# An RWKV-7 and GELU kernel: channel sums two heads per matmul, and another order of its first tasks

## The chip, the cores and the metric

The kernel runs on one core of a Trainium2 chip. The metric is the device time of one execution in microseconds, taken as the median of several runs. The engines are TensorE (PE, with its weight loads PEld), VectorE (DVE), ScalarE (ACT), GpSimd (POOL) and SyncE (SP), whose queue issues nearly all transfers between main memory and the core.

## The reference

An RWKV-7 recurrence over 768 steps for 4 batches and 8 heads of width 40, then an MLP with a quick GELU over the 3072 tokens (8 heads of 40 make 320 inputs, 2048 hidden):

```python
for t in range(S):
    y[:, :, t] = np.einsum('bhd,bhde->bhe', rt, state)
    Sa = np.einsum('bhde,bhe->bhd', state, at)
    state_decay = state * wt[:, :, None, :] - np.einsum('bhd,bhe->bhde', Sa, bt)
    state = state_decay + np.einsum('bhd,bhe->bhde', vt, kt)
...
x = np.ascontiguousarray(attn_out.transpose(0, 2, 1, 3)).reshape(B * S, H * D)
h = x @ w_in
g = h * (1.0 / (1.0 + np.exp(-1.702 * h)))
return (g @ w_out).astype(np.float32)
```

## The kernel before

The recurrence is worked in 24 units: 12 chunks of 64 steps, each for two pairs of batches (16 heads' worth of work per unit, b a batch of the pair). For each unit the logarithms of the decays w are summed over time, and exponentials of the sums scale a, k, b and r (`decay`, `prep`). Sums by time come from a matmul (`by_time`, tile ps_cum). Sums by channel come for the first four units (`BY_PE = 4`) from matmuls too (`by_channel`, tile ps_cumc), for the others from scans on VectorE over a second copy of w (tile wc). Then come products of the scaled factors (tiles ps_A, ps_N, ps_RV), the inverse of a triangular matrix in five levels (`inverse`: matmuls into ps_level, a copy on ScalarE or VectorE, L794, a transpose on VectorE, L733, and so on; the result is T), the solution and the state (`solve`: ps_B, ps_X, the product M on VectorE, ps_y, then x). x goes to main memory and comes back in another layout (x_dram, xT_all). Every two units give one chunk of the MLP (`mlp`): up-projections into ps_up, GELU on ScalarE, down-projections into ps_down.

The MLP's weights come as eight pieces of 1280 columns in 64-bit form, four transfers each, and are brought to 32 bits in the kernel (`weight`): a pass on ScalarE (L457), three on VectorE (L461, L465, L469), a join on GpSimd (L473). Their raw bytes land in places that other data uses later: extra, w_sb, xT_all.

All this is cut into 2709 tasks, and the string ORDER lists them by hand in one sequence: the number of the task, a letter for its engine (p, a, d, g, s), and for tasks that use PSUM a bank. Each engine takes its tasks in this order. For a transfer (s) the digit is a window: the queue waits until at most so many transfers, among all before, are still under way.

```python
def transfer(t, dst, src, queue=nc.sync):
    begun.append(queue.dma_start(dst, src).ins)
    if t.window and len(begun) > t.window:
        tc.add_manual_dep(begun[-1], begun[-1 - t.window].name, ...)
```

Tiles rotate: two buffers for a with k, b, r with v; three for the log decays (logw) and for wc. A load into a buffer waits for the readers of what was in it.

Of the kernel before, what the change touches and what calls it, by code (L numbers as in the profile page):

```python
# [109 lines left out]
0s 8s 1s4 5s 102a 7s 6s 3a 9s 157a 87p0 88p1 10s 89a1 100p2 90a0 95d 13s4 4a 11s 93d 12s 101d2 98p3 2s 94d 97d 17s 103p1 16s 96d  # L110
142p0 15s 104a1 105d1 141p2 143a0 106d 99d3 107p1 144a2 18s4 148g 132p3 108a1 109d1 155p0 45s4 149d 27s 150g 156d0 158p2 14s4
110p1 159a2 160d2 91s4 130p0 161d 19a 24s4 112d1 162p2 111a1 22d 26s4 25s 163a2 113p1 20d 131a0 152g 164d2 34s4 92a 272s 21d
165p0 114a1 151g 271s 147a 153p2 115d1 273s 166a0 167d0 116p1 23g 28a 154d2 262p0 343s 117d1 263p2 133a3 342s 264a2 118d1 168p3
36s 31d 33s 119p1 276g 169a3 170d3 35s 120d1 42s 122a1 171p2 277d 278g 121a 43s 124d1 123a1 126p3 173d2 125a1 127d3 285a 29d
128p1 172a2 44s4 286p3 30d 54s4 37a 174p2 129d1 32g 51s4 288d3 134p1 178a2 146s4 175d2 145s 265a0 135d1 176a 187p0 289d 136p1
275s4 179a2 266g 61s 38d 138d1 188a0 341s 139s 287a3 181p0 39d 185p3 40d 137a1 177a2 290p1 313d 180a2 182a0 53s4 280g 279g 274s
186a3 183p2 292d1 281p0 291a1 333p3 41g 184d2 332p1 282d0 189p2 334a3 60s4 345s 314p0 190d2 316a0 346d 355a 191p3 347d 315d0
193d3 356p2 344s2 62s 140s 194s 195s4 192d3 293p0 335a1 358d2 46a 283p3 359d 317p1 294a0 295d0 349g 318a1 284d3 360p0 269a 348d
350g 296p1 336d 361a0 362d0 319p3 383d 357a2 297a1 298d1 384p0 321p2 49d 320a3 299p1 385a0 47d 322a2 63s4 363p3 300a1 301d1
323d2 386a0 302p1 364a3 365d3 353p0 351p2 306a1 48d 267s3 207p3 52s3 307a1 305d1 208p3 50g 268s3 64a 303d1 209p3 352d2 210p3  # L120
211p3 354d0 308a1 196p2 304a 212p3 65d 197p2 213p3 72s3 214p3 70s3 270d 55a 309p1 337s3 198p2 69s4 366p0 310a1 66d 199p2 367a0
200p2 58d 468p1 201p2 368d0 469a 473s 202p2 476s 203p2 67d 387p0 477s 470a1 490d 204p2 68g 480s 339a 205p2 369p1 388d0 206a2
215p3 371d1 218p0 219p0 56d 472s4 216p3 483g 71s4 220p0 217a3 471d 81s4 221p0 482d 79s 311p2 222p0 370a1 223p0 224p0 312d2 225p0
340d 372p3 229p1 478s4 376a3 230p1 57d 378a3 324p2 560s4 377a3 59g 226p0 78s4 375a3 325d2 231p1 73a 232p1 227p0 373d3 326p2 374d
228a0 389p3 484g 479s3 327d2 338s4 240p0 529d 390a3 481g 328d2 379p3 233p1 380a3 329d 234p1 391p2 485g 241p0 556s4 392d2 80s4
242p0 393d2 74d 486p3 235p1 487d3 530p2 236p1 75d 531a2 381p3 237p1 532a2 330s4 382d3 238p1 76d 491p2 394p3 494a2 493d2 77g
239a1 243p0 395d3 82a 488p1 557s3 396p3 489d1 474a 558s4 83d 331s 251p1 492d2 495d 252p1 84d 85d 253p1 398d3 86g 559s4 548p2
244p0 703s 397d3 549a 570d 553s 245p0 496d 550a2 552s 399d 497a 254p1 551g 554a 498p3 564d 400s 568p2 565g 499a3 246p0 569d2
500d3 563g 247p0 562d 694p2 561g 255p1 248a0 401s2 249d0 475d 256p1 250s 533p3 257p1 534a3 555d 695a 571p0 535p3 573d0 258p1
574a0 698s4 501d 696a2 609d 502g 536a3 537p2 572d0 259a1 576d 566p3 538a2 702s 402p0 575g 567d3 577a 403p0 404p0 539d2 785s3  # L130
700a 405p0 706s 708d 406p0 578p3 407p0 580d3 408p0 260d1 610p2 409p0 581d 709g 410p0 611d2 411p0 612d2 503p1 707d 582g 412a0
424p2 425p2 504d1 704s2 426p2 505d1 427p2 697d 428p2 579d3 613p1 701d 429p2 614a1 583p0 430p2 584a0 506d 431p2 585d0 432p2 507a
782s2 586d 433p2 587d 446p3 434a2 508p1 588p0 509a1 447p3 590d0 589a0 510d1 261s2 413p2 511d 699s 414p2 591d 512a 783s 415p2
592g 416p2 513p0 417p2 514a0 515d0 593p1 516d 418p2 594a1 595d1 419p2 596d 420p2 517a 597d 421p2 422p2 518p0 423a2 435p1 519d0
436p1 521d0 520g 437p1 522d0 438p1 523d0 439p1 440p1 524d0 525p2 716p0 526a2 441p1 717d0 927s 442p1 718d0 527p2 443p1 719d0
444p1 528d2 598p0 721d 445a1 540p2 720d 722g 601d0 603a0 617p1 602d0 541d2 448p3 618a1 604d0 542p2 619d1 599d0 600d 615p1 705s
544d2 449p3 616a1 781s 710d 545g 711d 605p0 723p1 606a0 450p3 607p0 451p3 546s 608d0 930s 452p3 725d1 724d1 620p0 726d 543d2
727a 773p1 453p3 621d0 778s 774a 547s 754d 728p2 622p0 454d3 455d3 729d2 456s 457p3 775a1 776g 730d2 784s 786g 779a 777s 624d0
458p3 623d0 625g 731d 793p1 833d 732a 459p3 733p2 789g 460p3 626s 734a2 794d1 735d2 714p0 790g 736d 461p3 780d 737g 1009s 918p1
755p2 923s 462p3 715d0 756a2 627s 757a2 788d 463p3 738p0 787d 464p3 739a0 740d0 919a 795p2 465d3 758p0 1006s 466d3 798a2 921d  # L140
650p3 467s 759d0 920a1 651p3 924a 928s 796d2 712p1 797d2 652p3 922s 800d 799g 653p3 932d 801a 654p3 834p0 655p3 713d1 656p3
657p3 835d0 760p2 836d0 925d 658p3 761a2 659p3 762p1 660a3 741d 628p0 742d 926s 629p0 630p0 763d1 802p2 764d1 631p0 803a2 804d2
632p0 805d 633p0 806a 743p3 634p0 746d3 635p0 747d3 837p1 931g 748d3 636p0 838a1 1007s 749d3 637p0 807p2 744d3 933g 638a0 639p1
808d2 640p1 791p3 745a 809d2 672p0 810d 792d3 811a 750p2 641p1 751a2 812p3 642p1 813a3 814d3 752p2 643p1 753d2 644p1 815d 645p1
816a 765p3 839p2 766d3 646p1 840a2 647p1 817p3 648p1 818a3 819d3 767p2 820d 649a1 821d 673p0 769d2 929s 768d2 770g 822p3 934d
674p0 825a3 826a3 940p1 827a3 675p0 1151s 828a3 935d 943a1 771s 661p2 823d3 662p2 941d1 1154s 824a 663p2 942d1 997p3 945d 944g
664p2 998a 1002s 978d 938p1 946g 665p2 939d1 666p2 772s 667p2 668p2 829p1 669p2 999a3 1000d 1001s 830d1 670p2 1003a 1011d 676p0
671a2 1004d 831p3 841p1 677p0 832d3 1005s 842d1 936p3 843d1 678p0 937d3 844p2 679p0 845d2 947p1 1010g 680d0 846p3 948a1 681d0
1012d 682s 683p2 847d3 1013g 1008s 848d3 1019p0 1014g 949d1 684p2 1022a0 1230s 849d 1233s 979p3 685p2 980a3 950d 850s 1020d0
981a3 951g 1142p1 1021d0 686p2 1024d 1143a 1147s 1023d 1025g 982p3 1057d 687p2 1152s 952p0 851s 983a3 1145g 688p2 1156d 1146s  # L150
953a0 954d0 984p3 1144a1 955d 1148a 689p2 956d 985a3 1149d 986p0 690p2 987a0 1150s 988d0 957p1 691a2 863p3 958a1 692d2 864p3
959d1 865p3 693s 960d 866p3 961d 1026p0 867p3 1027a0 1028d0 868p3 1029d 1155g 869p3 1157d 1030a 1058p2 870p3 871p3 1059a2 872p3
# [97 lines left out]
def rwkv7_gelu_quick(ctx: ExitStack, tc: tile.TileContext, time_d, v_d, w_d, wc_d, ak_d, b_d, rv_d, w_in, w_out, out):  # L250
# [125 lines left out]
    for t in logw_t:  # L376
        nc.gpsimd.memset(t[:, DM:], 0.0)
# [772 lines left out]
```

## Time and profile before

| | us |
|---|---|
| median of 3 runs | 681.54 (681.05 to 681.87) |
| the profiled execution's own time | 679.49 |
| its span | 677.7 |
| TensorE busy | 649.6 (96%) |
| VectorE busy | 449.7 (66%) |
| ScalarE busy | 329.1 (49%) |
| GpSimd busy | 175.7 (26%) |
| mean granted TensorE clock | 0.994 of full |

The span runs from the first to the last instruction; the profiled execution is one run, and the 1.8 us between its time and its span lie around the instructions. Busy time of TensorE holds matmuls at whatever pace they run. Durations in the timelines are those of merged rows, so neighbouring rows of one engine overlap by their pipelining.

### The profile page before, as it was taken

The numbers are of one execution on the slowest core, as the hardware profiler recorded it, in microseconds if no ns is written. First come the engines' busy times: TensorE is split into PE (matmuls) and PEld (weight loads), VectorE is DVE, ScalarE is ACT, GpSimd is POOL, SyncE is SP. The second block draws the span as 40 slices with busy tenths as digits, with TensorE's granted clock in tenths as the row PEclk, the third lists the DMA queues.
The fourth block names the chain that finished last, engine by engine and source line by source line (L and its number), as shares of the span: only waits on it lengthen the run. The fifth ranks groups of instructions, "written<-read, shape, count | busy, mean of one in ns | idle before, by whom it ended". The sixth has DMA issues, their size and how long they took to land.

```text
span 677.7 us, 42447 instructions
## 1 busy us (share of the span) xinstructions
PE 649.6 (96%) x19616; PEld 568.7 (84%) x19616; DVE 449.7 (66%) x916; ACT 329.1 (49%) x681; POOL 175.7 (26%) x201
## 2 busy tenths in 40 slices
PE   5777999999999999999999999999999999999997
PEld 4667787787999997888888899999889798799896
DVE  5777779777867668757776687868656766675001
ACT  3676745634564655654545445455344454263010
POOL 6541443324123123123113211322411421300000
PEclk9979999999999999999999999999999999999999
DMA  6875753415324314432404513513412411200200
GB/s 208 295 255 160 226 172 97 129 42 152 107 64 131 94 58 124 114 107 65 124 14 131 149 35 108 155 33 107 140 38 62 130 53 45 69 15 14 60 13 21
DMA packets 35473, 69.74 MB, mean 103 GB/s; under 512 B 5472, under 2 KB 14816, under 8 KB 35296
## 3 DMA queue, kind: packets, MB, share of 16 engines
q1 hardware_dynamic: 35216, 66.99, 32.9%
q8 instruction: 154, 2.52, 1.6%
q14 instruction: 23, 0.19, 0.1%
q10 hardware_dynamic: 80, 0.04, 0.0%
HBM read 59.15 MB, written 7.86 MB: 99 GB/s over the span
## 4 chain that ended last, share of the span: by engine, by line
PE 88%; DMA 6%; DVE 2%; issue 1%; SPq 1%; ACT 1%; DVEq 0%; ACTq 0%
PE ps_up L301 31%; PE ps_down L301 29%; PE ps_level L301 8%; PE ps_y L301 5%; PE ps_B L301 4%; PE ps_X L301 2%; PE ps_N L301 2%; PE ps_rz L301 1%; PE ps_RV L301 1%; PE ps_A L301 1%; PE ps_zT L301 1%; SPq L331 1%; DMA w_sb<-in_w_in 1%; PE ps_cum L301 1%; PE ps_T L301 1%
## 5 line engine op out<-in xcount | busy, mean ns | idle before, releaser
L301 PE MATMUL ps_up<-xT_all,w_sb 64*64 64x256 f32 x3840 | 253.3, 377 | 2.1 <-issue 1.3
L301 PE MATMUL ps_down<-w_sb,g 64*64 64x320 f32 (+1 forms) x3200 | 241.5, 419 | 0.2 <-ACT zr L879 0.2
L301 PEld LDWEIGHTS ps_up<-xT_all,w_sb 64*64 64x64 f32 x3840 | 170.8, 133 | 18.8 <-issue 2.1
L301 PEld LDWEIGHTS ps_down<-w_sb,g 64*64 64x64 f32 x3200 | 142.5, 133 | 31.6 <-issue 0.4
L1000 ACT ACTIVATE g<-ps_up 128x1024 f32<-128x1024 f32 x48 | 49.2, 1025 | 46.3 <-PE ps_up L301 45.8
L719 POOL TENSOR_TENSOR EX<-ES,quads 128x512 f32<-128x512 f32 x30 | 39.7, 1324 | 116.4 <-DVE ES L712 77.7
L761 ACT COPY W<-ps_level 128x512 f32<-128x512 f32 x56 | 32.8, 585 | 67.7 <-PE ps_level L301 66.0
L301 PEld LDWEIGHTS ps_level<-W,EX 64*64 64x64 f32 x2560 | 60.0, 134 | 5.4 <-DVE T L840 0.2
L763 DVE TENSOR_TENSOR E<-two,ps_level 128x256 f32<-128x256 f32 x80 | 33.1, 415 | 36.5 <-ACT W L761 32.3
L301 PE MATMUL ps_level<-W,EX 64*64 64x64 f32 (+1 forms) x2560 | 56.8, 217 | 0.0
L717 ACT ACTIVATE EX<-ES,quads 128x256 f32<-128x256 f32 x82 | 37.2, 501 | 31.9 <-DVE ES L712 31.3
L629 POOL TENSOR_TENSOR ak<-ak,FT 128x512 f32<-128x512 f32 x17 | 23.0, 1353 | 77.2 <-DMA ak<-in_ak 54.4
L301 PEld LDWEIGHTS ps_level<-PT,EX 64*64 64x64 f32 x1280 | 30.7, 138 | 11.5 <-DVE EX L733 3.3
L301 PE MATMUL ps_level<-PT,EX 64*64 64x64 f32 (+2 forms) x1280 | 32.5, 234 | 6.9 <-DVE EX L733 5.0
L712 DVE STREAM_TRANSPOSE ES<-E 128x256 f32<-128x256 f32 x80 | 35.3, 443 | 4.4
L301 PE MATMUL ps_y<-RV,kh 64*64 64x104 f32 (+1 forms) x768 | 35.4, 247 | 0.9 <-DVE M L917 0.9
L301 PE MATMUL ps_y<-M,bh 64*64 64x104 f32 (+1 forms) x768 | 35.5, 247 | 0.7 <-DVE M L917 0.5
L901 ACT COPY B<-ps_B 128x416 f32<-128x416 f32 (+1 forms) x35 | 17.2, 493 | 34.4 <-PE ps_B L301 34.2
L301 PEld LDWEIGHTS ps_y<-RV,kh 64*64 64x64 f32 x768 | 29.6, 133 | 3.2 <-DVE M L917 1.5
L917 DVE TENSOR_TENSOR M<-ps_X,later 128x832 f32<-128x832 f32 (+1 forms) x24 | 23.9, 995 | 10.2 <-PE ps_X L301 10.0
L301 PE MATMUL ps_B<-RV,A 64*64 64x104 f32 (+1 forms) x768 | 29.2, 252 | 0.8 <-issue 0.8
L637 POOL TENSOR_TENSOR kh<-time,G 128x320 f32<-128x320 f32 x18 | 16.2, 901 | 51.2 <-PE ps_y L301 34.6
(133 smaller groups left out, 1099.0 us busy)
## 6 DMA issues: line engine op xcount, KB each, us to landing
ak<-in_ak SPq DMA_DIRECT2D x48, 160.0 KB
rv<-in_rv SPq DMA_DIRECT2D x48, 160.0 KB
time<-in_time SPq DMA_DIRECT2D x24, 320.0 KB
xT_all<-x_dram SPq DMA_DIRECT2D x48, 160.0 KB
wc<-in_wc SPq DMA_DIRECT2D x20, 264.0 KB
logw<-in_w SPq DMA_DIRECT2D x24, 160.0 KB
RV<-in_v SPq DMA_DIRECT2D x24, 160.0 KB
b<-in_b SPq DMA_DIRECT2D x48, 80.0 KB
```

What stands on the lines that cost most here:

```text
L301: nc.tensor.matmul(o, lhsT, rhs, start=start, stop=True, skip_group_check=True)
L331: begun.append(queue.dma_start(dst, src).ins)
L629: plan.add(R, {"DVE": 690.0, "POOL": 1270.0, "sbuf": True}, lambda t: of(t.engine).tensor_mul(ahT(), ahT(), FT_of(i)), reads=T("ak", "FT") ...
L637: plan.add(R + 4, {"POOL": 870.0, "DVE": 490.0, "sbuf": True}, lambda t, n=n, dst=dst: of(t.engine).tensor_mul(dst(i)[:, :, :D], by_head(t ...
L712: plan.add(rank, dve(256), lambda t: nc.vector.transpose(ES(n), source(t)), writes=[key("ES", n, 6)], **reads)
L717: nc.scalar.activation(dst[:, :, h], ES(n), ACT.Copy, scale=quads[:, h, :1])
L719: of(t.engine).tensor_mul(dst, ES(n).unsqueeze(2).to_broadcast([128, 8, 2, 32]), quads.unsqueeze(1).to_broadcast([128, 8, 2, 32]))
L761: plan.add(rank, any2(512), lambda t: copy(t.engine)(tiles_of(W(n + 1)), blocks(psum(t, ""), 64)), writes=[key("W", n + 1, 5)], pair=pair)
L763: plan.add(rank, dve(256), lambda t: nc.vector.tensor_sub(tiles_of(E(n + 1)), every(two32, [128, 2, 4, 32]), blocks(psum(t, ""), 64)[:, :, ...
L901: plan.add(R, any2(4 * wide), lambda t: copy(t.engine)(dst(), some(psum(t, "")[:, :, :208])), writes=[("Bv", i)] if x and c > 0 else T("B" ...
L917: plan.add(R + 1, dve(8 * wide), lambda t: nc.vector.tensor_tensor(M_of(i)[:, :, :wide].rearrange("p (j b) n -> p b j n", b=2), some(psum( ...
L1000: plan.add(-45, {"ACT": 1030.0, "table": "gelu"}, lambda t: nc.scalar.activation(g_of(c * NQ + q).rearrange("p m r n -> p r m n"), psum(t, ...
```

## The change

Three things change together. For the first four units the log decays are loaded from a new array in which each head's 40 columns are padded to 64 with ones, into the wc buffer, which these units don't use otherwise. The logarithm is taken of the 40 columns of each head only. `by_channel` then takes 128 columns (two heads) as weights of one matmul, 8 per unit in place of 16, each writing all 128 partitions. The padding columns of logw and their three memsets go. And the first 1227 of the 2709 entries of ORDER are written anew: 96 tasks change their engine, many their bank, the transfers their order and windows (before: none, 2, 3 or 4; after: none, 2, 3, 4, 6 or 8). On TensorE the order differs up to its 345th task.

```diff
 ORDER = """
-0s 8s 1s4 5s 102a 7s 6s 3a 9s 157a 87p0 88p1 10s 89a1 100p2 90a0 95d 13s4 4a 11s 93d 12s 101d2 98p3 2s 94d 97d 17s 103p1 16s 96d
...
+0s6 157a 9s8 5s 6s 3a 88p0 8s 102a 87p2 89a0 1s 4a 14s 93d 94d 10s6 90a2 2s8 92a 95d 96g 103p1 105d1 104d1 97g 7s6 98p2 99d2
...
...
-    logw_t = several("logw", [128, DM + 24])
-    for t in logw_t:
-        nc.gpsimd.memset(t[:, DM:], 0.0)
+    logw_t = several("logw", [128, DM])
...
-    logw_of = lambda i: logw_t[i % 3][:, :DM]
+    logw_of = lambda i: logw_t[i % 3] if i >= BY_PE else apart(i).rearrange("p (h d) -> p h d", h=H)[:, :, :D]
+    apart = lambda i: wc_of(i).rearrange("p n h -> p (n h)")[:, :H * 64]
     def load_w(i):
-        for name, of, src, n in (("wc", wc_of, wc_d, 528), ("logw", logw_of, w_d, DM))[i < BY_PE:]:
+        for name, of, src, n in (("wc", wc_of, wc_d, 528), ("logw", logw_of, w_d, DM)) if i >= BY_PE else (("wc", apart, apart_d, H * 64),):
...
-                 reads=[("logw", i)] + ([("wc", i)] if i >= BY_PE else []) + ([("exps", i - 2)] if i > 1 else []), writes=[("log", i)])
+                 reads=[("wc", i)] + ([("logw", i)] if i >= BY_PE else []) + ([("exps", i - 2)] if i > 1 else []), writes=[("log", i)])
         def sums(t):
...
         def by_time(t):
-            ps, lw = psum(t, "ps_cum"), logw_of(i)
+            ps, lw = psum(t, "ps_cum"), logw_of(i) if i < BY_PE else logw_of(i).rearrange("p (h d) -> p h d", h=H)
             for n in (1, 0):
                 for b in BITS:
-                    mm(ps[HALF[u], b, :160], incl[HALF[b]], lw[HALF[b], n * 160:(n + 1) * 160], True)
-        plan.add(R, pe((1, 160)), by_time, reads=T("log"), uses=T("logw"), room=T("G"), writes=T("cum"), pair=("cum", i))
+                    mm(ps[HALF[u], b, :160].rearrange("p (h d) -> p h d", d=D), incl[HALF[b]], lw[HALF[b], 4 * n:4 * n + 4], True)
+        plan.add(R, pe((1, 160)), by_time, reads=T("log"), uses=T("logw") if i >= BY_PE else T("wc"), room=T("G"), writes=T("cum"), pair=("cum", i))
         def by_channel(t):
             for u, f in product(BITS, BITS):
-                for b, e in QUARTERS:
-                    o, h = (2 * u + f) * 65, head(e, f, b, u) * D
-                    mm(ps[HALF[e], b, o:o + 65], logw_t[i % 3][HALF[b], h:h + 64], edges[HALF[b]], o == 0)
+                for b in BITS:
+                    o, h = (2 * u + f) * 65, head(0, f, b, u)
+                    mm(ps[:, b, o:o + 65], apart(i)[HALF[b], 64 * h:64 * h + 128], edges[HALF[b]], o == 0)
         def exp_of_product(t):
...
-            plan.add(R, pe((4, 65)), by_channel, reads=T("log"), uses=T("logw"), room=T("FT", "GT"), pair=("cumc", i))
+            plan.add(R, pe_wide((4, 65)), by_channel, reads=T("log"), uses=T("wc"), room=T("FT", "GT"), pair=("cumc", i))
         def exp_channel(t):
...
+    by_time = time_tile(w, False)
+    apart = np.ones((4, 128, H, 64), np.float32)
+    apart[..., :D] = by_time[:4].reshape(4, 128, H, D)
     arrays = {
-        "in_w": time_tile(w, False),
+        "in_w": by_time,
+        "in_apart": apart.reshape(4, 128, H * 64),

```

More of the change, by code (lines that the diff above doesn't have):

```diff
@@ L114 @@
[L114 to L117, printed above, removed]
```

268 lines of the change are left out of this document (136 added, 132 removed).

## The prediction

> **What bounds the kernel now.** I read the page first: the span, the busy shares, the slices.
>
> ```profile
> span 677.7 us, 42447 instructions
> PE 649.6 (96%) x19616; PEld 568.7 (84%) x19616; DVE 449.7 (66%) x916; ACT 329.1 (49%) x681; POOL 175.7 (26%) x201
> PE   5777999999999999999999999999999999999997
> DMA  6875753415324314432404513513412411200200
> ```
>
> TensorE works 96% of the span, and its missing tenths lie in the first four slices (17 us each) and the last. Then the table by stretches (us, busy PE, PEld, DVE, ACT, POOL with instruction counts, granted clock, DMA share, GB/s), cut at the first matmul of the MLP (66.5 us):
>
> ```profile
> 0.00:66.50 66.50, 45.52 (x1705) 40.14 (x1706) 46.79 (x81) 40.14 (x103) 28.50 (x54) 0.95 0.72 228
> 66.50:120.00 53.50, 52.08 (x1413) 41.93 (x1408) 43.96 (x72) 31.02 (x62) 24.54 (x15) 1.00 0.54 168
> 120.00:300.00 180.00, 179.15 (x5555) 157.00 (x5551) 128.86 (x268) 99.05 (x203) 47.95 (x51) 1.00 0.34 100
> ```
>
> The opening leaves TensorE idle for 66.50 - 45.52 = 21.0 us; the next stretches leave 1.4 and 0.85 us. From 66.5 us on the kernel is bound by matmuls, so whatever brings the first MLP matmul forward brings the end forward, if nothing behind it then arrives late. The change reorders the opening, and 21.0 us is more than it can win there: the four first units are chains (level matmuls, a copy on ScalarE, a transpose on VectorE, the next level), and a chain waits on itself. Third, the timelines of the opening (start, duration, engine, what; in brackets idle time before it and what ended that), TensorE first:
>
> ```profile
> 3.80 0.81 PE L301 MATMUL ps_cum<-logw,edges 64*64 64x160 f32 x8 [3.80 <-POOL logw L377]
> 8.91 1.02 PE L301 MATMUL ps_RV<-rv 40*64 40x64 f32 x27 [0.59 <-DMA rv<-in_rv]
> 11.71 1.13 PE L301 MATMUL ps_N<-b,ak 40*64 40x64 f32 x32 [0.82 <-DVE b L631]
> 19.29 0.76 PE L301 MATMUL ps_N<-b,ak 40*64 40x64 f32 x29 [1.03 <-DMA extra<-in_w_in]
> 23.55 0.89 PE L301 MATMUL ps_level<-PT,EX 64*64 64x96 f32 x32 [0.28 <-ACT PT L794]
> 42.00 0.41 PE L301 MATMUL ps_y<-RV,kh 64*64 64x104 f32 x8 [0.91 <-DVE M L917]
> 64.82 0.67 PE L301 MATMUL ps_level<-PT,EX 64*64 64x32 f32 x32 [0.84 <-DVE EX L733]
> 66.48 2.48 PE L301 MATMUL ps_up<-xT_all,w_sb 64*64 64x256 f32 x40
> ```
>
> These are the milestones: N of unit 0 at 11.71, N of unit 1 at 19.29, the third level of unit 0 (L4 in what follows) at 23.55, y of unit 0 at 42.00, the last level of unit 2 at 64.82, the first up-projection at 66.48. The last follows that level, RV and A of unit 3 without a gap, so TensorE's own queue, not the arrival of x, releases it.
>
> **The change part by part.** *Channel sums with two heads per matmul.* Per unit 16 matmuls of 64 rows by 64 columns become 8 of 64 by 128, four units only (each matmul stands twice in the trace, 32 records per unit).
>
> ```profile
> 4.36 1.12 PE L301 MATMUL ps_cumc<-edges,logw 64*64 64x65 f32 x32
> 47.30 0.65 PE L301 MATMUL ps_cumc<-edges,logw 64*64 64x65 f32 x32
> 3.57 0.23 POOL L377 MEMSET logw<- 128x24 f32 x3
> 3.19 0.47 ACT L536 ACTIVATE logw<-logw 128x320 f32<-128x320 f32 x1
> ```
>
> A unit costs 0.65 us, or 1.12 us early on. Half the records, each over twice the columns: at best half the time, a gain of 2 x 1.12/2 + 2 x 0.65/2 = 1.8 us over four units, at worst twice the time, a loss of 3.5 us. I take nothing: the 64 columns of weights that a record loses, the other gains, and it streams the same 65 columns. The cover is the opening's idle TensorE (32% of it); without it the ends above would count. No row shows a matmul of 64 by 128 beside the 64 by 64 ones, so the switch between them is among the unknowns. [...]
>
> The three memsets on GpSimd (0.23 us) leave the front of TensorE's first work, which waited for them until 3.80. In their place the first load is 256 KB instead of 160. The load issued first had landed before 3.19; the first stretch of the run moves too little to say more than that 96 KB at the 228 GB/s of the opening are 0.4 us. Ln then starts near 3.6 and ends near 4.1 instead of 3.66, and the channel sums, now ahead of the time sums, start at about 4.1 to 4.3 instead of 4.36. No gain, no loss. The four padded loads add 0.38 MB, 1.7 us of the stream at that rate, spread over the opening.
>
> *The loads in another order.* Issued by the time TensorE reaches its 30th task: 56 transfers, 11.8 MB before, 40 transfers, 8.9 MB after (counted off the two lists). What unit 0 needs first (decays, k and b, a and k, b) goes first; r and v wait.
>
> ```profile
> 6.97 0.69 DVE L634 TENSOR_TENSOR ak<-ak,GT 128x512 f32<-128x512 f32 x1 [2.28 <-DMA ak<-in_ak]
> 10.16 0.69 DVE L660 TENSOR_TENSOR RV<-ps_RV,upper 128x512 f32<-128x512 f32 x1 [1.87 <-PE ps_RV L301]
> 10.77 0.68 DVE L631 SCALAR_TENSOR_TENSOR b<-b,GT 128x512 f32<-128x512 f32 x1
> 9.45 0.35 SPq L331 DMA_DIRECT2D RV<-in_v  x1
> ```
>
> N of unit 0 needs scaled a and b. Scaled b (10.77) stood on VectorE behind the mask of RV (10.16), which waited for r and v by way of the matmul at 8.91. In the new order RV comes five tasks of TensorE later. The issue at 9.45 was held until b (1.28 MB into the list) had landed; a and k (0.80 MB) had landed by 6.97. That is 0.48 MB in 2.5 us, so b at 1.06 MB should land near 8.3 and a and k, at 0.90, near 7.5: two products of 0.7 us, N at about 9.0, 2.7 us sooner. The new order puts padded decays of unit 1 and 2 ahead of other work on ScalarE, where Ln of unit 2 waits for its load (2.4 MB into the list) with the exponentials of unit 1 behind it; these start near 14 us, when they do now, so N of unit 1 comes at 16.5 to 17, 2 to 3 us sooner.
>
> But that lead meets a gate. On ScalarE the first pass over the MLP's weights (L457) stands ahead of the copies of the next levels, in both orders:
>
> ```profile
> 20.44 1.40 ACT L457 ACTIVATE w_sb<-extra 128x1280 f32<-128x1280 f32 x1
> 22.70 1.50 ACT L794 COPY PT<-ps_level 128x768 f32<-128x768 f32 x2 [0.86 <-DVE EX L733]
> 33.55 0.91 ACT L717 ACTIVATE T<-ES,quads 128x256 f32<-128x256 f32 x2
> 37.00 1.41 ACT L457 ACTIVATE w_sb<-w_sb 128x1280 f32<-128x1280 f32 x1 [0.38 <-DMA w_sb<-in_w_in]
> ```
>
> It began at 20.44. The pieces of that weight end 4.45 MB into the new list, 4.00 MB into the old: 0.45 MB at 228 GB/s would be 2.0 us later, while the windows (how many transfers may be under way) of 6 and 8 instead of 4 keep the stream fuller from 5 to 13 us and could pay all of it back. With the pass at 20.4 the copy at 22.70 comes near 21.8 and L4 near 22.5, **1.0 us** sooner; the ends are 2.7 sooner and 1.0 later.
>
> From L4 (23.55) to y of unit 0 (42.00) ScalarE loses work to other places: the pass over the third weight (37.00, 1.41 us) goes behind the levels of unit 2; the two spreads of T (0.91 us each) go to GpSimd; it gains one copy of 0.75 us (half the 1.50 above). Net 2.5 us less on an engine whose copies alternate with levels on the chain; the three passes over that weight on VectorE go with it. The spreads are slower on GpSimd:
>
> ```profile
> L719 POOL TENSOR_TENSOR EX<-ES,quads 128x512 f32<-128x512 f32 x30 | 39.7, 1324 | 116.4 <-DVE ES L712 77.7
> ```
>
> 1.32 us against 0.91 costs unit 0, whose spread is on the path, 0.4 us. So 2.5 - 0.4, about **2.0 us** sooner (ends: nothing, if levels and not copies set the pace, and 4). The third term is x. Its path on the load queue now:
>
> ```profile
> 54.86 1.72 SPq L331 DMA_DIRECT2D xT_all<-x_dram x2
> 56.67 0.84 SPq L331 DMA_DIRECT2D x_dram<-x  x2
> 61.39 1.09 SPq L331 DMA_DIRECT2D xT_all<-x_dram  x2
> 52.43 0.86 DVE L962 TENSOR_TENSOR x<-ps_y,FT 128x128 f32<-128x128 f32 x4
> ```
>
> x of unit 1 is done at 53.29 and its store goes out at 56.67, 3.4 us later, because the reload of unit 0's x sat ahead of it. In the new order that reload stands three loads further ahead. The reload of unit 1 then has five transfers (two with a window of 3) between store and itself, but it waits 4.7 us for the store today anyway. So x can be there 3 us sooner, which is no gain by itself and lets the 3 us above count. Sum: 1.0 + 2.0 = **3.0 us**, first up-projection near 63.5.
>
> **After the first up-projection** the weights have to come in time; the orders are alike in kind up to TensorE's 345th task and the same after it. In 120 to 300 us there is 0.85 us to win and any amount to lose; I take nothing. The profiled execution took 679.49 us, 1.8 around its span; the forecast for it is 676.5, and for the median of the runs, 681.54, which lies 2.05 above it, 681.54 - 3.0 = 678.5.
>
> **The rivals.**
>
> *A half clock avoided.* Two windows and one row of the timeline:
>
> ```profile
> 30.00:35.00 5.00, 3.03 (x119) 2.41 (x119) 3.96 (x8) 3.73 (x16) 2.99 (x2) 1.00 0.93 314
> 35.00:41.00 6.00, 5.28 (x136) 4.89 (x136) 3.64 (x8) 4.73 (x11) 3.13 (x2) 0.50 0.93 303
> 32.80 0.89 PE L301 MATMUL ps_level<-PT,EX 64*64 64x96 f32 x32 [1.03 <-DVE EX L733]
> ```
>
> After a stretch 61% busy the granted clock is 0.50 from 35 to 41 us, and 5.28 us of matmuls there would have been 2.6 at full clock. If the denser new order escapes it, up to 2.6 us more are won: 678.5 - 2.6 = 675.9. Against it: the new order still has gaps of the same kind. [...]
>
> *No gain.* The pass over the first weight comes 2 us late for the 0.45 MB, eats the lead, and the copies taken off ScalarE were not what the chain waited for: 681.5.
>
> *Slower: the weight of the first down-projection comes late.*
>
> ```profile
> 88.47 0.44 PE L301 MATMUL ps_down<-w_sb,g 64*64 64x320 f32 x3
> 83.97 2.99 POOL L473 TENSOR_TENSOR w_sb<-w_sb,xT_all 128x1280 int32<-128x1280 int32 x1 [2.95 <-DVE w_sb L465]
> SPq L331 <- DMA extra<-in_w_out: 11.3, 6, 4.3
> ```
>
> Today that weight is joined at 86.96, 1.5 us ahead of the first ps_down at 88.47. Its last piece is listed with the first up-projection task; in the new order two of four pieces are listed 14 and 17 TensorE tasks after that one, roughly 8 us, with up to 4.3 us to land (the longest wait of the queue for such a piece); then ScalarE 1.4, VectorE three times 0.8, GpSimd 3.0: 19 us if no queue holds it. But its passes stand on VectorE behind products of y of unit 2, and its join behind a product of unit 4; that puts the join near 26 us after the first up-projection, while the 39 up-projection tasks (0.46 us each, 40 records taking 2.3) and some nine us of other matmuls ahead of ps_down make 27. The margin is 1 us. If those products are 4 us late, TensorE, which takes its queue in order, stands 3 us, the weights behind it (each through the same three engines) stand likewise, and with an opening that won 1 us the sum is 2 us slower, 683.5. It decides from the point at which the join ends later than TensorE reaches ps_down.
>
> **How the numbers follow.** Forecast 0.45: 678.5, its own range 676.5 to 680.2 from the ends of the two terms. Half clock avoided 0.13: 675.9. No gain 0.10: 681.5. Slower 0.32: 683.5, from 682.9 to 686. A measurement of this kernel can tell about 0.2%, 1.4 us, from no change. Faster 0.58, same 0.10, slower 0.32. The range, 674.8 to 684.5, leaves out one in ten at each side: 675.9 less a first term at its good end, and the slower case beyond one more microsecond.
>
> **What would show it.** N of unit 0 near 9 us and of unit 1 near 17; the first L457 on ScalarE near 20.4; y of unit 0 near 39 and the first ps_up near 63.5 us; idle TensorE before it near 18 us; the gaps from 66 to 120 us still about 1.4 us. ps_cumc as 16 records of 64 rows by 128 columns in 0.65 us or so. I am wrong if the first pass over the weights comes after 22 us, if the first ps_up is not ahead of 65, or if TensorE stands for a weight (a wait of ps_up or ps_down on GpSimd's joins) after it.

## Result: slower by 0.64%, and the profile after

The changed kernel takes 687.84 us (median of 18 runs, 680.28 to 690.86), the kernel before 682.05 us in the same job (18 runs, 679.09 to 686.15): 0.85% more by the medians. The ratio used from here on, 1.0064 (95% interval 1.0037 to 1.0090), leaves out two of the changed kernel's runs that were in the chip's slower state, and lies near the ratio of the means of the others (1.0061). Forecast were 678.5 us and a range of 674.8 to 684.5. Its profiled execution took 685.41 us, 2.4 us under its median; that of the kernel before, 679.49, lies 2.6 under the median here. Runs of one kernel lie up to 11 us apart, so what a profile shows is first of all a reading of one execution.

The lines of the page after that answer to those of before (span, busy shares, TensorE and DMA in 40 slices):

```profile
span 683.7 us, 42287 instructions
PE 656.4 (96%) x19552; PEld 568.8 (83%) x19552; DVE 450.9 (66%) x922; ACT 322.7 (47%) x670; POOL 176.2 (26%) x200
PE   5877999999999999999999999999999999999997
DMA  7778643424414414332404513513411411200200
```

TensorE has 64 matmuls less and 6.8 us more busy time, which is more than the 6.0 us of the span. The timelines of the opening, TensorE first, then ScalarE's first pass over the weights:

```profile
9.26 1.19 PE L301 MATMUL ps_N<-b,ak 40*64 40x64 f32 x30 [2.53 <-DVE b L630]
17.42 1.15 PE L301 MATMUL ps_N<-b,ak 40*64 40x64 f32 x29 [0.88 <-ACT PT L793]
22.46 0.89 PE L301 MATMUL ps_level<-PT,EX 64*64 64x96 f32 x32
39.84 0.25 PE L301 MATMUL ps_y<-RV,kh 64*64 64x104 f32 x1
65.42 0.62 PE L301 MATMUL ps_level<-PT,EX 64*64 64x32 f32 x32
66.13 0.81 PE L301 MATMUL ps_up<-xT_all,w_sb 64*64 64x256 f32 x8
...
20.35 1.38 ACT L455 ACTIVATE w_sb<-extra 128x1280 f32<-128x1280 f32 x1 [0.53 <-DMA extra<-in_w_in]
```

N of unit 0 is 2.45 us ahead of before, N of unit 1 1.87, L4 1.09, y of unit 0 2.16. The last level of unit 2 is 0.60 behind, and the first up-projection only 0.35 ahead. That last milestone is not the same point in the two kernels. After:

```profile
66.58 0.81 PE L301 MATMUL ps_RV<-rv 40*64 40x64 f32 x31
67.81 0.27 PE L301 MATMUL ps_RV<-rv 40*64 40x64 f32 x1 [0.42 <-issue]
68.73 0.46 PE L301 MATMUL ps_A<-ak 40*64 40x64 f32 x19
```

RV and A of unit 3, which came ahead of the first up-projection before, stand behind its first matmuls now. A fair point is the first up-projection of the second chunk, by which both have done the same matmuls but for the wide form and 32 short ones: 120.35 us before, 121.60 after. Cut there (us, then busy time and counts by engine, granted clock, DMA share, GB/s), before first:

```profile
0.00:120.35 120.35, 97.95 (x3129) 82.42 (x3132) 90.75 (x152) 71.34 (x165) 53.40 (x69) 0.97 0.64 201
120.35:677.69 557.34, 551.66 (x16501) 486.32 (x16492) 358.95 (x764) 257.73 (x517) 122.34 (x133) 1.00 0.28 82
```

```profile
0.00:121.60 121.60, 102.22 (x3096) 88.11 (x3100) 91.75 (x155) 66.15 (x152) 58.48 (x72) 0.97 0.65 195
121.60:683.70 562.10, 554.22 (x16471) 480.70 (x16462) 359.16 (x768) 256.57 (x518) 117.73 (x128) 1.00 0.29 83
```

Up to that point the new kernel leaves TensorE idle 3.0 us less (19.4 against 22.4), about the gain forecast for the first up-projection, but keeps it busy 4.3 us longer for the same work. Behind it 4.8 us more are lost, the part that I took at nothing. The lag is 1.26 us at this point, 0.34 at the fourth chunk's first up-projection (226 us), 2.71 at the fifth's (279 us) and 6.0 at the end. TensorE's order differs up to its 345th task, which lies in the fourth chunk: 3.3 us of the 6.0 are lost where it is the same.

Of the 4.3 us, 2.6 are the wide channel sums. The groups of before and after (count | busy, mean ns | idle):

```profile
L301 PE MATMUL ps_cumc<-edges,logw 64*64 64x65 f32 x128 | 3.6, 267 | 0.1
```

```profile
L301 PE MATMUL ps_cumc<-edges,wc 64*128 64x65 f32 x64 | 6.2, 350 | 4.0 <-ACT wc L535 4.0
```

Another 0.7 us is what the low clock may have added, by an estimate: both kernels have 6.8 us of it in the opening, filled with 5.37 us of matmuls before and 6.82 after, and half the difference is 0.7. Of the last 0.9 us the 32 short matmuls are a part (32 of ps_A take 0.46 us from start to start); the rest stays open.

Behind the opening, gaps appear inside groups of equal matmuls, where nothing is waited for that the profile shows ("issue"). Two of them in the timeline of after:

```profile
236.79 0.39 PE L301 MATMUL ps_level<-W,EX 64*64 64x64 f32 x10 [0.80 <-issue]
240.64 0.24 PE L301 MATMUL ps_level<-W,EX 64*64 64x32 f32 x2 [0.84 <-issue]
```

Summed over TensorE from the second chunk's first up-projection to the end, such gaps are 0.64 us before and 3.19 after. They have a pattern. Instructions come by DMA, in two queues by the pages (154 and 23 packets). The larger, the same in both pages, I take for TensorE's by the count below:

```profile
q8 instruction: 154, 2.52, 1.6%
```

2.52 MB in 154 packets are 16 KB a packet. TensorE's records of the kernel before, 39232 matmuls and weight loads and 287 of its sequencer (semaphores and drains), over 154 are 256.6: one packet brings a block of 256 instructions. Counting these records in order, all five issue gaps over 0.3 us before and seven of eight after lie at record 190 to 198 of a block of 256; over all kernels below it is 129 of 145. I read them as TensorE standing until code comes; e4 and e8 below bear that out. The gaps are a part of it only: behind the fifth chunk's first up-projection they are 0.8 us more than before (1.12 against 0.28). But the time from one matmul's start to the next, summed there over the records 188 to 201 of each block, 14 of 256, is 25.9 us after and 23.2 before, while over all records it is 3.1 us more: most of what is lost there is lost at the boundaries. The wide form takes out 128 instructions, half a block, so that every boundary behind the opening falls on other code.

### The profile page after: what moved, and what is told of

It reads as the page before. It is cut to its first block, busy times and chain, and to the rows that moved or that the text cites. A ratio compares the mean times of both kernels' runs of the same rounds, so it can differ in the third digit from the quotient of the medians.

```text
span 683.7 us, 42287 instructions
## 1 busy us (share of the span) xinstructions
PE 656.4 (96%) x19552; PEld 568.8 (83%) x19552; DVE 450.9 (66%) x922; ACT 322.7 (47%) x670; POOL 176.2 (26%) x200
## 3 DMA queue, kind: packets, MB, share of 16 engines
q8 instruction: 154, 2.52, 1.6%
## 4 chain that ended last, share of the span: by engine, by line
PE 88%; DMA 5%; ACT 2%; issue 2%; DVE 1%; SPq 0%; POOL 0%; DVEq 0%; ACTq 0%
PE ps_down L301 29%; PE ps_up L301 28%; PE ps_level L301 9%; PE ps_y L301 5%; PE ps_B L301 4%; PE ps_X L301 2%; PE ps_N L301 2%; PE ps_RV L301 1%; PE ps_rz L301 1%; PE ps_A L301 1%; DMA b<-in_b 1%; PE ps_zT L301 1%; DMA extra<-in_w_out 1%; PE ps_cum L301 1%; PE ps_T L301 1%
## 5 line engine op out<-in xcount | busy, mean ns | idle before, releaser
L301 PEld LDWEIGHTS ps_up<-xT_all,w_sb 64*64 64x64 f32 x3840 | 169.0, 134 | 22.2 <-issue 2.0
L301 PEld LDWEIGHTS ps_down<-w_sb,g 64*64 64x64 f32 x3200 | 144.1, 133 | 33.0 <-issue 0.4
L716 ACT ACTIVATE EX<-ES,quads 128x256 f32<-128x256 f32 x76 | 34.5, 500 | 28.4 <-DVE ES L711 28.0
L301 PEld LDWEIGHTS ps_level<-PT,EX 64*64 64x64 f32 x1280 | 33.3, 148 | 6.0 <-ACT PT L793 1.4
L301 PE MATMUL ps_level<-PT,EX 64*64 64x64 f32 (+2 forms) x1280 | 35.4, 246 | 2.7 <-DVE EX L732 1.2
L628 POOL TENSOR_TENSOR ak<-ak,FT 128x512 f32<-128x512 f32 x16 | 20.9, 1304 | 55.4 <-DMA ak<-in_ak 43.3
```

What stands on the lines that cost most here:

```text
L301: nc.tensor.matmul(o, lhsT, rhs, start=start, stop=True, skip_group_check=True)
L628: plan.add(R, {"DVE": 690.0, "POOL": 1270.0, "sbuf": True}, lambda t: of(t.engine).tensor_mul(ahT(), ahT(), FT_of(i)), reads=T("ak", "FT") ...
L716: nc.scalar.activation(dst[:, :, h], ES(n), ACT.Copy, scale=quads[:, h, :1])
```

## The experiments

**The edit in two halves, and half a block put back.** The first four kernels separate the wide sums, the order, and the place of the boundaries. The unused matmuls are 4 instructions a call (two matmuls, two weight loads):

```diff
+    idle = banks.tile([128, 2, 512], FP32, tag="pair3", name="ps_idle")
+    for n in range(32):
+        r, q = QUARTERS[n % 4]
+        mm(idle[HALF[q], r, n // 4 * 8:n // 4 * 8 + 8], full[HALF[r], :64], full[HALF[r], 64:72], True)
     tasks = plan.listed(ORDER)
```

e1 is the changed kernel with the ORDER of before:

> The changed kernel's padded loads and channel sums of two heads per matmul, with the task order of the kernel before. It has 128 TensorE instructions fewer than the kernel before, like the changed kernel, so the 256-instruction blocks in which TensorE's code arrives begin at other tasks. Theory A (the loss is in the wide matmuls and in which tasks the block boundaries fall on; the new order by itself gains): wide matmuls at 2.0 and 1.1 us a unit in place of 1.1 and 0.65, some 1.5 us of it on the path, and some 2.5 us of mid-group stalls after 230 us: 4 us slower than the kernel before, near 686. Rival B (the new order itself costs, by late weights or x): within 1.5 us of the kernel before. Rival C (what the pair of profiles shows after 230 us is chance or traffic of transfers): only the 1.5 us of the wide matmuls, 683.5, and the stalls after 230 us no longer than in the kernel before.

e2 is the changed kernel with the narrow sums of before:

```diff
-                for b in BITS:
-                    o, h = (2 * u + f) * 65, head(0, f, b, u)
-                    mm(ps[:, b, o:o + 65], apart(i)[HALF[b], 64 * h:64 * h + 128], edges[HALF[b]], o == 0)
+                for b, e in QUARTERS:
+                    o, h = (2 * u + f) * 65, head(e, f, b, u)
+                    mm(ps[HALF[e], b, o:o + 65], apart(i)[HALF[b], 64 * h:64 * h + 64], edges[HALF[b]], o == 0)
```

> The changed kernel (new order, padded loads) with channel sums as 16 matmuls of 64 by 64 per unit, as before. TensorE has as many instructions as in the kernel before. Theory A: the four sums take 1.1 and 0.65 us again, the first up-projection comes 2 to 3 us ahead of that of the kernel before (near 64), the lag after 230 us doesn't grow, and the time is 1 to 3 us under the kernel before, near 680. Rival B (the order costs): 3 to 5 us above the kernel before, with waits of ps_up or ps_down for weights or x. Rival C: the first up-projection near 64, and no forecast after it better than that of the kernel before.

e3 and e4 are the changed kernel and the kernel before, each with the 128 instructions:

> The changed kernel with 32 small calls of unused matmuls (8 columns; 128 TensorE instructions) ahead of the first task, into a PSUM bank that is written over later; nothing else differs. The block boundaries fall where they fell in the kernel before. Theory A: the dummies cost at most some 2 us of the time in which TensorE waits for the first load anyway, the stalls inside groups after 230 us shrink from some 3 us to some 0.6, and the time is 2 to 3 us under the changed kernel. Rivals B and C: the same time as the changed kernel or up to 1 us more, with stalls after 230 us as long as there.

> The kernel before with the same 128 unused TensorE instructions ahead of the first task, so that its block boundaries fall where those of the changed kernel fall. Theory A: stalls inside groups after 230 us grow by 2 to 3 us, and the time is 2 to 4 us above the kernel before, near 685. Rivals B and C: the time of the kernel before, at most 1 us more for the dummies.

Measured, beside 681.63 us of the kernel before: e1 686.63 (ratio 1.0078, 1.0053 to 1.0103), e2 688.88 (1.0118, 1.0078 to 1.0159), e3 691.23 (1.0156, 1.0118 to 1.0193), e4 688.31 (1.0100, 1.0064 to 1.0136). Theory A holds for e1 in time, and for e4 in direction: nothing but 128 unused instructions cost 6.7 us, where it gave 2 to 4. It falls for e2 and e3: the order alone is 7.2 us slower with the boundaries of before, and putting these back made the changed kernel slower still. But the later part went as forecast for all four: from 280 us to the end the lag behind the kernel before grew by 4.4 us in e1 and 2.8 in e4 (after: 3.3), and by -0.3 and 0.3 in e2 and e3. What I had missed is that boundaries cost most in the opening. The timeline of e4:

```profile
27.41 0.27 PE L301 MATMUL ps_level<-PT,ident 64*64 64x128 f32 x1
30.84 0.69 PE L301 MATMUL ps_level<-PT,ident 64*64 64x128 f32 x5 [3.16 <-issue]
```

A gap of 3.16 us, with no semaphore behind it, in the middle of a group of eight. The page of the DMA from 28.4 to 29.6 us in e4 holds one fetch of code, which starts at 28.50; in the 1.2 us ahead of that there is none, while data move at 235 GB/s from 27.2 to 31 us:

```profile
q8 instruction: 1, 0.02, 5.6%
```

TensorE goes on 2.34 us after the fetch began. Behind the halt the granted clock is low for 13 us, twice the 6.8 us that the kernel before shows in its whole opening:

```profile
30.50:43.50 13.00, 11.41 (x303) 10.73 (x306) 8.38 (x15) 7.76 (x24) 4.90 (x3) 0.50 0.84 272
```

That the halt brought the low clock about is likely and not shown; in their profiles the kernels of this document have from 3.4 us (e1) to 34 us (e15) of it in the opening, without a rule that I could find. What it can be worth follows from the clocks of all runs: the mean granted clock is 0.9888 in e4 and 0.9932 in the kernel before beside it. If TensorE was busy all of that time, e4 loses 3.0 us more to the clock (an estimate; 2.4 for e2, 2.9 for e3, nothing for e1). So the low clock can be part of e4's 6.7 us, and not all of it.

**The same block, a whole block, and traffic.** e5 is e1 with the 128 instructions, e6 is e2 with them; e7 is the kernel before with 256, half of them behind TensorE's second task; e8 has unused transfers late in the kernel before:

```diff
-    for t in tasks:
+    for n, t in enumerate(tasks):
         t.fn(t)
+        if 1600 <= n < 2600 and t.engine == "SP":
+            for k in range(2):
+                spare = dram.tile([128, 2 * DM], FP32, tag=f"spare{n}_{k}", name="spare")
+                nc.sync.dma_start(spare[:], time_d[k])
```

> Order of the kernel before, padded loads, wide channel sums, and 128 unused TensorE instructions ahead of the first task, so that from the fourth unit on TensorE's 256-instruction blocks begin where they do in the kernel before. Theory D (TensorE stands at block boundaries: the next block's fetch starts 0.3 to 3.7 us after the last boundary and the code can run some 2.3 to 2.9 us after that start, while a block of small dense matmuls lasts only some 3.3 us; which groups the boundaries fall on and what transfers are under way then set the loss): the lag behind the kernel before doesn't grow after 280 us, where it grew by 2.7 to 4 us in the three kernels with the other boundaries; the whole 1.5 to 4 us above the kernel before, below the wide sums without the 128. Rival E (the unused instructions by themselves cost some 5 us, or only the transfers' luck differs): 5 us above the wide sums without them, near 691.

> New order, padded loads, narrow channel sums (16 matmuls of 64 by 64), and 128 unused instructions, so that the blocks begin as in the changed kernel from the fourth unit on. Theory D: the lag grows by 2.5 to 4 us after 280 us as in the changed kernel; the opening stalls differ from those of the new order without the 128 (7.5 us up to 72 us) and can only be fewer by luck; 686 to 692. Rival B (the new order costs whatever the boundaries): 688 or more with the stalls at block boundaries no longer than in the kernel before. Rival E: 5 us above the new order without the 128, near 694.

> The kernel before with 256 unused TensorE instructions (128 ahead of the first task, 128 behind the second, where TensorE waits for a load): a whole block, so that every boundary falls on the same task as in the kernel before. Theory D: within 2 us of the kernel before, the lag flat after 280 us, stalls at block boundaries near 6 us in all as there. Rival E (the instructions themselves cost): 7 us or more above the kernel before, no better than with 128.

> The kernel before with unused transfers from main memory to main memory (two of 320 KB after each transfer of the list between entries 1600 and 2600, some 420 to 650 us); nothing waits for them. Theory D, if the fetch's late start is a wait behind data: the stalls inside TensorE's groups at block boundaries between 420 and 650 us, 0.3 us in the kernel before, become 3 us or more without a semaphore wait, and the time is as much longer. Rival F (the fetch is not slowed by data; its start is fixed by TensorE): these stalls stay below 1 us, and the time changes only where loads come late, which semaphore waits would show.

Measured beside 681.79: e5 685.57 (1.0049, 1.0021 to 1.0078), e6 690.35 (1.0133, 1.0092 to 1.0174), e7 682.96 (1.0016, 0.9993 to 1.0040), e8 742.7 (1.0855, 1.0787 to 1.0924). e7 against e4 is the cleanest pair: 256 unused instructions cost nothing that can be told, 128 cost 1.0%. It is not the instructions, it is where the boundaries fall. At the place where e4 stood 3.16 us, e7 doesn't stop:

```profile
27.16 0.40 PE L301 MATMUL ps_level<-PT,ident 64*64 64x128 f32 x8
27.90 0.50 PE L301 MATMUL ps_cum<-logw,edges 64*64 64x160 f32 x8 [0.34 <-DVE EX L733]
```

e8 shows what a late fetch hangs on. The stretch from 420 to 600 us, before first, then with traffic (columns as above), and one row of its timeline:

```profile
420.00:600.00 180.00, 179.06 (x5541) 158.28 (x5536) 121.65 (x252) 81.47 (x174) 48.59 (x53) 1.00 0.28 81
```

```profile
420.00:600.00 180.00, 144.81 (x4036) 126.14 (x4027) 91.55 (x187) 64.08 (x144) 35.75 (x39) 0.91 0.75 259
...
503.36 0.84 PE L301 MATMUL ps_X<-B,T 64*64 64x104 f32 x27 [2.65 <-issue]
```

TensorE gets through 27% fewer matmuls. From 400 us on the issue gaps at block boundaries are 17.2 us where the kernel before has 0.1 us. The mean time from one boundary to the start of the next fetch is 2.1 us there, 0.75 before; the time from that start to the end of a halt stays as it is, median 2.4 us in e8 and 2.5 over 108 halts of the other kernels. So the fetch is late because data are under way, and rival F falls. Not all of e8's excess, 58 us by the ratio, is this: in the profiled execution, at 746.35 us the longest of four, the clock is down to 0.91 in that stretch, loads of x come late, and two gaps of 8.7 and 7.5 us ahead of up-projections, put down to issue, lie at no boundary; I can't say what ended them.

e8 also shows how much one profile can tell. Up to its first unused transfer, at 388.44 us, its code, its boundaries and its loads are those of the kernel before. Yet from the second chunk's first up-projection to there it has 3.5 us of issue gaps, all at block boundaries, against 0.6 before, and its lag grows from 1.0 us at the second chunk to 4.2 at the fifth. The first of these gaps, at a boundary where the kernel before doesn't stop:

```profile
128.01 0.37 PE L301 MATMUL ps_up<-xT_all,w_sb 64*64 64x256 f32 x1 [1.32 <-issue]
```

So the same boundary halts one execution and not another, and 3 us between two profiles can be no more than that. What belongs to the code must come from the medians of many runs, or from a pattern over many kernels.

e5 and e6 speak on both sides. In e5 the lag stays flat after 280 us (-0.8), as theory D (halts where the boundaries fall) has it, and grows by 2.4 in e6, just under its 2.5 to 4. But the order stays slow in e6, with issue gaps after the second chunk of 2.48 us, against 0.64 in the kernel before: rival B, by its time, fares no worse than D.

**Other places of the boundaries, and the windows.** The same unused instructions, another number of them (in e10 half of them behind TensorE's second task); and the windows of the new list capped:

```diff
-        if t.window and len(begun) > t.window:
-            tc.add_manual_dep(begun[-1], begun[-1 - t.window].name, ...
+        if t.window and len(begun) > min(t.window, 4):
+            tc.add_manual_dep(begun[-1], begun[-1 - min(t.window, 4)].name, ...
```

> The changed kernel with 64 unused TensorE instructions ahead of the first task; every boundary of its 256-instruction blocks falls 64 instructions earlier in the code. Theory D (the boundaries decide): the time differs by some us from the changed kernel's (5.8 above the kernel before) and from that with 128 (9.6 above), in either direction, and a shift that beats the kernel before can exist. Rival B (the new order and the wide sums cost some 5 us wherever the boundaries fall): 4 to 8 us above the kernel before for each of the shifts.

> The changed kernel with 192 unused TensorE instructions (96 ahead of the first task, 96 behind the second). Theory D: another time again, in either direction, by as much as the stalls at block boundaries differ. Rival B: 4 to 8 us above the kernel before.

> The kernel before with 64 unused TensorE instructions ahead of the first task. Theory D: with a whole block the time was 0.16% above the kernel before, with half a block 1.0%; a quarter moves the boundaries too, and as the kernel before lies lowest of all that ran, 2 to 6 us above it is likelier than a gain. Rival B, by which the shift does nothing to the order before: within 1.5 us.

> The changed kernel with the windows of its transfers capped at 4 (they were 6 or 8 for some transfers of the opening); TensorE's code is the same, so the boundaries are too. If deep windows delay the fetch of code in the opening: fewer stalls up to 120 us, 1 to 3 us faster than the changed kernel. If the windows pay by bringing loads sooner: the first pass over the weights later than 20.4 us, and 0.5 to 3 us slower than the changed kernel.

Measured beside 682.79: e9 687.15 (1.0057, 1.0030 to 1.0084), e10 687.87 (1.0076, 1.0048 to 1.0104), e11 686.28 (1.0060, 1.0034 to 1.0086), e12 691.38 (1.0103, 1.0057 to 1.0149). e11 confirms D for the order before. For the new order rival B is met in both. e12: the deep windows seem to pay, 0.4% by ratios whose intervals overlap. With the cap the first pass over the weights comes at 22.93 us in place of 20.35, and the reload of x comes late for the first up-projections (3.6 us of TensorE's idle time ends with it, none in the changed kernel's opening), though the issue gaps up to the second chunk fall from 1.31 to 0.54.

**The last three.**

> The kernel before with 192 unused TensorE instructions (96 ahead of the first task, 96 behind the second). The same code at other shifts was 0 (a whole block: 0.16% above), 0.6% (a quarter) and 1.0% (half). Theory D: 2 to 6 us above the kernel before; with it the order before stands at all four quarters, and its mean over them is near 3.5 us above, against 6.2 for the changed kernel: some 3 us of the change's loss would be the edit and some 3 the place of the boundaries. Rival B (the edit costs all of it): within 1.5 us of the kernel before.

> The kernel before with 224 unused TensorE instructions, an eighth of a block short of a whole one. A count over the trace of before (blocks of 256 in a stretch shorter than the fetch takes) has its smallest sum of stalls here, 1.7 us under that of the present shift. Theory D with a fixed time of the fetch: 1 to 2 us faster than the kernel before. If the fetch's time hangs on the transfers of the moment, that count says little: 0 to 5 us slower.

> New order with narrow channel sums and 64 unused instructions: against the changed kernel with 64 only the form of the channel sums differs up to the first unit's; from the fourth unit on the boundaries fall as in the changed kernel with 192. If the wide form costs what its rows show (2.6 us of TensorE, two thirds of it on the path), 1 to 2 us faster than that one, 685 to 686; if the boundaries outweigh it, anywhere from 683 to 691.

Measured beside 682.56: e13 684.75 (1.0032, 1.0001 to 1.0064), e14 682.70 (1.0015, 0.9989 to 1.0042), e15 689.00 (1.0117, 1.0074 to 1.0160). e13 lies 2.2 us above the kernel before, at the low end of theory D's 2 to 6. e14's gain did not come: the count with a fixed fetch time has no use. e15 was to be faster than e10, whose boundaries it shares from the fourth unit on, if the wide form costs; it is no faster.

All together, as the excess in per cent over the kernel before in the same job; "shift" is the number of unused instructions:

| shift | order before, narrow | order before, wide | new order, narrow | new order, wide |
|---|---|---|---|---|
| 0 | 0 | 0.78 (e1) | 1.18 (e2) | 0.64 (the change) |
| 64 | 0.60 (e11) | | 1.17 (e15) | 0.57 (e9) |
| 128 | 1.00 (e4) | 0.49 (e5) | 1.33 (e6) | 1.56 (e3) |
| 192 | 0.32 (e13) | | | 0.76 (e10) |
| 224 / 256 | 0.15 (e14) / 0.16 (e7) | | | |

Three readings. The kernel before goes up to 1.0% and down again over one block, and it lies at the bottom. The order costs at equal shift and form 1.18, 0.57, 0.33, -0.14 and 1.07: 0.6% on average, 4 us. The wide form, with the boundaries behind the opening equal (wide at 0 beside narrow at 128, 128 beside 0, 192 beside 64), costs -0.22 and 0.49 in the order before and -0.69, 0.38 and -0.41 in the new one: nothing on average. Over the four quarter shifts the order before stands at a mean of 0.48 and the changed kernel at 0.88 (apart by 0.64, -0.03, 0.56 and 0.44). So some 0.4% (2.7 us) of the change's 0.64 is the edit wherever the boundaries fall, with intervals of 0.3 on each entry; that the rest is the place that the kernel before happened to have is how I read the table, not a measurement of its own. No version beats the kernel before.

The profiles show where the order's share lies (us from the traces; gaps put down to issue, summed):

| kernel | second chunk begins | issue gaps to there | from there to the end | issue gaps there |
|---|---|---|---|---|
| before | 120.35 | 2.81 | 557.34 | 0.64 |
| before + 256 (e7) | 122.33 | 3.98 | 558.24 | 0.62 |
| before + 192 (e13) | 120.50 | 5.68 | 559.15 | 1.25 |
| before + 64 (e11) | 128.73 | 9.64 | 555.98 | 0.19 |
| before + 128 (e4) | 124.25 | 7.54 | 561.06 | 0.91 |
| the change | 121.60 | 1.31 | 562.10 | 3.19 |
| the change + 64 (e9) | 122.66 | 2.12 | 563.24 | 4.45 |
| the change + 192 (e10) | 128.06 | 3.65 | 562.00 | 3.43 |
| the change + 128 (e3) | 127.97 | 7.39 | 560.67 | 2.19 |
| new order, narrow (e2) | 128.67 | 9.34 | 559.31 | 2.44 |

Each row is one execution. All eight kernels with the new order have over 2 us of issue gaps behind the second chunk, and of the seven with the old order and narrow sums only e8 has over 1.25; but its 3.5 us ahead of the first unused transfer show that the order before can halt as much, so the split is a strong pattern and not a rule. Behind 280 us it is the place of the boundaries that the lag follows: in the five kernels with the late boundaries of the changed one (it, e1, e4, e6, e12) it grows there by 1.4 to 4.4 us, in the ten others but e8 by -1.5 to 1.5. In e2, where the boundaries of before are back, they lie ahead of 280 us: of its lag of 10.3 us, 8.3 are there at the second chunk and 10.6 at the fifth. So the order's share seems to lie in the first 280 us, in the opening's halts and in those behind it. There both the engines' order and the list of loads (to its 1227th entry) are new. Which of the two brings the halts stays open: the new loads under the old order of the engines weren't tried.

## Why the prediction was wrong, point by point

- *What bounds the kernel.* Partly right. It is matmuls after 66 us, but "from 66.5 us on bound by matmuls" left out the 1.7 us of issue gaps that were in the trace of before (1.04 of them from 66 to 120 us) and that an edit of the code can multiply.
- *The loads; N of unit 0 near 9.0, of unit 1 at 16.5 to 17.* Nearly right: 9.26 and 17.42.
- *The gate: first pass at 20.4, L4 near 22.5.* Right to 0.05 us: 20.35 and 22.46. The term of 1.0 us measured 1.09.
- *From L4 to y of unit 0, 2.0 us.* Mis-sized: y came 2.16 us sooner, 1.07 beyond L4's lead. And even the 1.07 can't be credited to the copies taken off ScalarE. Before, the low clock lay in this stretch, with 5.37 us of matmuls in it, worth up to 2.7 us by the working of my own rival; after, the granted clock is 1.00 there. The spreads of T, moved to GpSimd, I priced by their duration (0.4 us); TensorE waits 1.03 and 1.54 us for them, where it waited 0.60 us for one before. The second wait stands just ahead of y:

```profile
39.09 0.46 PE L301 MATMUL ps_Q<-T,P 64*64 64x64 f32 x16 [1.54 <-POOL T L718]
```

- *The first ps_up near 63.5.* This is the step of the opening that failed; it came at 66.13, and not ahead of 65 was one of my signs of being wrong. I moved the lead of y to the first up-projection without following what stands between, and held TensorE's busy time fixed. The windows from the one to the other, before first:

```profile
42.00:66.48 24.48, 18.78 (x848) 16.94 (x849) 19.03 (x36) 15.36 (x39) 6.52 (x5) 1.00 0.58 168
```

```profile
39.84:66.13 26.29, 20.63 (x769) 19.44 (x759) 18.75 (x34) 12.12 (x31) 10.69 (x9) 0.87 0.83 238
```

  The new places of the work made new waits:

```profile
42.90 0.40 PE L301 MATMUL ps_T<-QT,Tc 64*64 64x64 f32 x11 [0.95 <-ACT Tc L806]
48.17 0.41 PE L301 MATMUL ps_y<-RV,kh 64*64 64x104 f32 x8 [1.02 <-ACT G L600]
54.56 0.69 PE L301 MATMUL ps_rz<-rv,zT 40*64 40x64 f32 x32 [1.20 <-ACT P L701]
61.28 0.89 PE L301 MATMUL ps_level<-PT,EX 64*64 64x96 f32 x32 [1.22 <-DVE EX L732]
```

  But they only replace others: TensorE is idle 5.7 us in both. It is busy 1.85 us longer, with 79 matmuls fewer, at a granted clock of 0.87 against 1.00. The low clock, ahead of y in the kernel before, now lies here, with 6.82 us of matmuls in it (up to 3.4 us, an estimate), and one unit's wide sums add 0.46. Up to the first up-projection TensorE's idle time is 17.9 us, the 18 that I forecast; its busy time grew from 45.50 to 48.24. And the milestone itself moved: RV and A of unit 3, 0.9 us ahead of the first up-projection before, went behind it.
- *Wide matmuls at nothing, between -1.8 and +3.5.* Mis-sized in the rows: +2.6 us, near the upper end, 1.98 us for 16 records where 32 narrow ones took 1.12, and 1.11 against 0.65 to 0.69 late. Yet the table shows no cost of the form in the time; it takes 128 instructions off the fetches as well. Which of these weighs what in the opening stays open. Nor do the rows show a price for the switch between the two forms: each record is longer (350 ns against 267), and TensorE goes on without a gap behind three of the four groups (behind the fourth it waits 0.19 us, put down to VectorE).
- *After the first up-projection, nothing.* This is the step that failed most: 4.8 us in the profiled pair. I argued from an order alike in kind, and then equal, to equal time. TensorE's code came in other blocks, and the fetches of these fell on other work and other loads: 3.3 us went where the order is the same, most of it at the boundaries, and the four other kernels with these late boundaries lose 1.4 to 4.4 us there too. The part ahead of that, 1.5 us, is within what two executions of the same code differ by (3.2 us there in e8).
- *The rivals.* The half clock: 6.8 us at 0.50 in both kernels, so in sum it was not escaped; it moved from ahead of y to behind it. The late weight of the first down-projection, my slower case: ps_down came 5.2 us later (93.70), but no gap of TensorE in that chunk ends with a join, so the mechanism did not decide. The slower outcome had 0.32 for another reason than the true one, and ended at 686, short of the 687.84 measured.
- *The sums.* From the ends of the two terms (1.0 later to 2.7 sooner, nothing to 4) follow 674.8 to 682.5, not 676.5 to 680.2, and 675.9 less the first term's good end is 674.2, not 674.8. Neither reaches what was measured.

Single crossings of a block's boundary cost up to 3.16 us in this kernel, and moving their place by 128 unused instructions made it 6.7 us slower (e4).

## What to carry to other kernels

In this kernel TensorE's code is a stream of transfers (2.52 MB in 154 fetches), and a fetch began on average 2.1 us after a boundary beside e8's traffic, 0.75 us in the kernel before. So where TensorE runs many small matmuls, look in the trace for gaps inside groups that nothing ends, count their records modulo 256, and try to have heavy loads beside long matmuls, not beside dense short ones (argued from e8, not tried). Before an edit that changes the number of instructions is judged, run it, and the kernel before, at a few shifts of unused instructions; otherwise the measurement is of the edit and of a new draw of boundaries together. And compare two orders at a point by which both have done the same work.

## What the hardware showed that was not expected

- TensorE halts at boundaries of 256 instructions: 129 of the 145 issue gaps over 0.3 us lie at record 190 to 198 of a block, up to 3.16 us long (e4); that it waits there for the next block is my reading. The fetch began 0.75 to 2.1 us after the last boundary on average (in the kernel before, and in e8 with traffic at 259 GB/s), and code ran 2.2 to 3.4 us after it began, with the traffic (median 2.4) as without (2.5); the quickest blocks of dense small matmuls last 3.0 to 3.3 us, so there is next to no room for a delay. The same boundary can halt one execution and not the next: e8 and the kernel before, equal up to 388 us, have 3.5 and 0.6 us of such halts between the second chunk and there.
- Unused transfers on which nothing waits made a kernel 58 us slower (e8), with at least 17 us of it in such halts.
- A matmul of 64 rows by 128 columns of weights over 65 columns is no saving over two of 64 by 64: 16 of them take 1.7 times as long as 32 narrow ones (over four units 6.2 us for 64 against 3.6 for 128).
